# Reordering a two-layer feed-forward stage: upper half of d_ff first, differences cut at a quarter, attention of the next block at later slots

## The chip, the cores and the metric

The kernel runs on one core of a Trainium2 chip. The metric is the time on the device in microseconds (us), taken as the median of several executions. The profile is one such execution seen by the hardware profiler; its span is a little shorter than the time (290.2 us against 291.96 us for the same execution).

The engines are named as in the profile: PE is the matrix engine (PEld is its loading of weights), DVE the vector engine, ACT the scalar engine, POOL the general engine, SP the engine whose queue issues most of the transfers.

## The reference, cut to what matters

Attention inside chunks of 64 rows, and behind it a feed-forward layer with a squared relu:

```
q, k, v: (8, 8, 576, 64)          # batch, heads, sequence, head size
scores = q_chunk @ k_chunk^T / 8  # 64 x 64 for each chunk
attn   = exp(scores - max) / sum
out    = attn @ v_chunk
x = out as (4608, 512)            # tokens, d_model
h = max(x @ w_in, 0)              # w_in  (512, 2048)
y = (h * h) @ w_out               # w_out (2048, 512)
```

Everything comes in as float32; the kernel multiplies in bfloat16 and sums in float32.

## The kernel before

The 4608 tokens are cut into nine blocks of 512, numbered j = 0 to 8; each block consists of two groups of 256 tokens. Blocks 2 to 8 share one form, and the change touches only that form. Such a block is a chain of 30 slots on PE:

- slots 0 to 15: the first layer. In a slot PE multiplies one tile `ft` (128 of the 2048 hidden units) for all 512 tokens, in 4 matmuls of 512 columns; ACT takes the relu, and DVE (for some tiles ACT) squares it into `gT[:, ft, :]`, the left factor of the second layer.
- slots 16 to 29: the second layer, as seven products of half-size blocks in place of eight (a scheme of Strassen's kind). Two slots of 8 matmuls make one product. Some products need `gT` itself, others need a difference of two quarters of it, which DVE forms.

The four quarters of `gT`, by hidden units and tokens, and the differences of them:

```python
def quarters(j):       # a11, a12, a21, a22
    return [gTs[j][:, a:a + HF, c:c + HT] for c in (0, HT) for a in (0, HF)]
# HF = 8 tiles of hidden units, HT = 256 tokens:
# a11: ft 0-7,  tokens 0-255     a12: ft 8-15, tokens 0-255
# a21: ft 0-7,  tokens 256-511   a22: ft 8-15, tokens 256-511
DIFFERENCES = {"d1": (0, 3), "d2": (3, 2), "d5": (0, 1), "d6": (2, 0), "d7": (1, 3)}
EARLY_DIFFERENCES = {8: "d5", 12: "d2"}

def difference(j, name, part):     # part: which of the 8 tiles
    ...
    nc.vector.tensor_tensor(out=state[name, j][:, part], in0=x, in1=y, op=ALU.subtract)

FT_PAIRS = [ft + h for ft in range(n_ft // 2) for h in (n_ft // 2, 0)]
#        = 8, 0, 9, 1, 10, 2, ... 15, 7
```

The first layer. `u` counts the slots, `ft` is the tile of that slot:

```python
for u, (c, n, fts, ft) in enumerate(...):
    h = ps_ffn.tile([128, 512], FP32, name="ps_ffn")          # 4 buffers
    for dt in range(n_dt): nc.tensor.matmul(out=h[:, 0:n], ...)
    ...
    rl = ffn_pool.tile([128, 512], FP32, name="rl", bufs=3)   # bf16 for j < 3
    nc.scalar.activation(out=rl[:, 0:n], in_=h[:, 0:n], func=AF.Relu)
    on_act = SQUARES_ON_ACT_PAIRS if fts is FT_PAIRS else SQUARES_ON_ACT   # (9, 11, 5)
    if (n == 512 and ft in on_act) or ...:
        nc.scalar.activation(out=gT[:, ft, c:c + n], in_=rl[:, 0:n], func=AF.Square)
    else:
        nc.vector.tensor_tensor(out=gT[:, ft, c:c + n], in0=rl, in1=rl, op=ALU.mult)
    if fts is FT_PAIRS and u in EARLY_DIFFERENCES:
        difference(j, EARLY_DIFFERENCES[u], slice(0, HF // 2))
    yield
```

The second layer. `rest_of` forms what is still missing of a difference. The seven products run through two banks of `ps_ffn`, called "n" and "m":

```python
def rest_of(name):
    difference(j, name, slice(HF // 2 if (name, j) in state else 0, HF))
d5 = rest_of("d5")
d2 = rest_of("d2")
yield from product("n", a22, b11_p_b21, True)     # slots 16, 17
... nc.scalar.copy(out=n1, in_=ps)                # ACT
yield from product("m", a11, b12_p_b22, True)     # slots 18, 19
... add(nc.vector, w, ps, n1)                     # DVE
d1 = rest_of("d1")
yield from product("n", d5, b22, False)           # slots 20, 21
... nc.scalar.copy(out=n2, in_=ps)
d6 = rest_of("d6")
yield from product("m", d2, b11, False)           # slots 22, 23
... add(nc.vector, c21, w, ps, ALU.subtract), store
d7 = rest_of("d7")
yield from product("n", d1, b11_m_b22, False)     # slots 24, 25
...
yield from product("m", d6, b11_p_b12, False)     # slots 26, 27
...
yield from product("n", d7, b21_p_b22, False)     # slots 28, 29
```

Between the slots the attention of the next block is woven in, in a plan of slots for its two groups: `SC` scores (64 small matmuls on PE for the two groups, one exponential each on ACT), `AV` values (32 small matmuls in two tiles, and on DVE for each tile a reciprocal and a multiplication), `XT` the transpose of the result by a transfer, `C` and `TD` the cast and transpose of q and k for the block after the next. What is planned at a slot is issued after the relu and square of that slot.

```python
slots = {SC: (6, 6), AV: (9, 13), XT: (12, 16), C: (18, 20), TD: (20, 23)}   # blocks 5, 6, 7
if j == 3:   slots.update({SC: (8, 8), AV: (10, 14), XT: (13, 17)})
elif j == 4: slots.update({SC: (7, 7), AV: (10, 14), XT: (13, 17)})
if j == 2:   slots = {SC: (8, 10), AV: (12, 15), XT: (15, 18), C: (20, 23), TD: (22, 25)}
```

Both `SC` and `AV` use `ps_att`, a pool of 2 buffers: a tile of `AV` waits until the exponential, or the multiplication of the tile two before it, has read its buffer. Block 8 is the last and has no attention woven in.

Of the kernel before, what the change touches and what calls it, by code (L numbers as in the profile page):

```python
# [17 lines left out]
def kernel(  # L18
# [18 lines left out]
    n_ft = d_ff // 128  # L37
# [15 lines left out]
    FIRST_DMA_T = 4  # L53
    FIRST_DMA_X = 6
    SQUARES_ON_ACT = (10, 14, 3)
    SQUARES_ON_ACT_PAIRS = (9, 11, 5)
    BT = GT * max(len(b) for b in blocks)

    const_pool = ctx.enter_context(tc.tile_pool(name="const", bufs=1))
# [132 lines left out]
    state = {}  # L192
# [159 lines left out]
    C, TD = cast_qk, transpose_qk_dma  # L352
    SC, AV, XT = scores, values, transpose_x
# [17 lines left out]
    gTs = {}  # L371
    HF, HD, HT = n_ft // 2, d_model // 2, BT // 2
    DIFFERENCES = {"d1": (0, 3), "d2": (3, 2), "d5": (0, 1), "d6": (2, 0), "d7": (1, 3)}
    EARLY_DIFFERENCES = {8: "d5", 12: "d2"}

    def quarters(j):

        return [gTs[j][:, a:a + HF, c:c + HT] for c in (0, HT) for a in (0, HF)]

    def difference(j, name, part):  # L380
        if (name, j) not in state:
            state[name, j] = wst_pool.tile([128, 1024], FP32, name="w_st").bitcast(BF16).rearrange(
                "p (a f) -> p a f", a=HF)
        x, y = (quarters(j)[i][:, part] for i in DIFFERENCES[name])
        nc.vector.tensor_tensor(out=state[name, j][:, part], in0=x, in1=y, op=ALU.subtract)  # L385
    FT_ORDER = [*range(n_ft // 2, n_ft), *range(n_ft // 2)]

    FT_PAIRS = [ft + h for ft in range(n_ft // 2) for h in (n_ft // 2, 0)]

    def ffn_in(j, parts):  # L390
        if j not in gTs:
            gTs[j] = ffn_pool.tile([128, n_ft, BT], BF16, name="gT")
        gT, xT = gTs[j], xTs[j]
        for u, (c, n, fts, ft) in enumerate((*p, ft) for p in parts for ft in p[2]):
            h = ps_ffn.tile([128, 512], FP32, name="ps_ffn")
            for dt in range(n_dt):
                nc.tensor.matmul(  # L397
                    out=h[:, 0:n],
                    lhsT=w_in_bf[:, dt, ft * 128:(ft + 1) * 128],
                    rhs=xT[:, c // 128:(c + n) // 128, dt, :],  # L400
                    start=(dt == 0), stop=(dt == n_dt - 1))
            if j < 3:
                if n == 512 or u % 2 == 0:
                    rl_tile = ffn_pool.tile([128, 512], FP32, name="rl", bufs=3).bitcast(BF16)
                rl = rl_tile[:, u % 2 * 512:] if n < 512 else rl_tile
            else:
                rl = ffn_pool.tile([128, 512], FP32, name="rl", bufs=3)
            nc.scalar.activation(out=rl[:, 0:n], in_=h[:, 0:n], func=AF.Relu)  # L408
            on_act = SQUARES_ON_ACT_PAIRS if fts is FT_PAIRS else SQUARES_ON_ACT
            if (n == 512 and ft in on_act) or (n < 512 and (j == 0 or ft in (12, 3))):  # L410
                nc.scalar.activation(out=gT[:, ft, c:c + n], in_=rl[:, 0:n], func=AF.Square)  # L411
            else:
                nc.vector.tensor_tensor(  # L413
                    out=gT[:, ft, c:c + n], in0=rl[:, 0:n], in1=rl[:, 0:n], op=ALU.mult)
            if fts is FT_PAIRS and u in EARLY_DIFFERENCES:
                difference(j, EARLY_DIFFERENCES[u], slice(0, HF // 2))
            yield


# [9 lines left out]
    def sum_quarters(out, in0, in1, op=ALU.add, half=slice(None)):  # L429
        return lambda _: add(nc.vector, out[:, half], in0[:, half], in1[:, half], op)  # L430

    def ffn_out(j):
# [6 lines left out]
        a11, a12, a21, a22 = quarters(j)  # L439

        def rest_of(name):
            difference(j, name, slice(HF // 2 if (name, j) in state else 0, HF))
            return state[name, j]

        n_tt = HT // 128
# [55 lines left out]
        d5 = rest_of("d5")  # L501
        d2 = rest_of("d2")
# [8 lines left out]
        d1 = rest_of("d1")  # L511
# [4 lines left out]
        d6 = rest_of("d6")  # L516
        if j == 1:
            d7 = rest_of("d7")
# [5 lines left out]
        if j > 1:  # L524
            d7 = rest_of("d7")
# [19 lines left out]
    def ffn_out_by_ft(j):  # L545

        gT = gTs.pop(j)
        n_tt = len(blocks[j]) * GT // 128
        o_ps = [ps_ffn.tile([128, d_model], FP32, name="ps_ffn") for _ in range(n_tt)]

        def mm(tt, ft):
            nc.tensor.matmul(  # L552
                out=o_ps[tt],
                lhsT=gT[:, ft, tt * 128:(tt + 1) * 128],
                rhs=w_out_bf[:, ft, :],
                start=(ft == 0), stop=(ft == n_ft - 1))


        for ft in range(n_ft - 4):
            for tt in range(n_tt - 1 if ft == 0 else n_tt):  # L560
                mm(tt, ft)
                if ft == 1 and tt == n_tt - 2:
                    mm(n_tt - 1, 0)
            yield
        for tt in range(n_tt):
            for ft in range(n_ft - 4, n_ft):
                mm(tt, ft)
            o_sb = ffn_pool.tile([128, d_model], FP32, name="o_sb", bufs=4)
            nc.scalar.copy(out=o_sb, in_=o_ps[tt])
            b, s0 = chunks[blocks[j][tt // 2]][0]  # L570
            t0 = b * S + s0 + tt % 2 * 128
            nc.gpsimd.dma_start(out=out[t0:t0 + 128, :], in_=o_sb)
            yield
# [49 lines left out]
    for j, grps in enumerate(blocks):  # L623
        nxt = blocks[j + 1] if j + 1 < len(blocks) else []
        far = blocks[j + 2] if j + 2 < len(blocks) else []
        plan = {}

        def at(slot, f, g):
            plan.setdefault(slot, []).append((f, g))

        if j == 0:
            loads, go_slots = itertools.chain(*map(qk_pieces, far)), range(17)
            at(28, sum_quarters(b11_p_b21, b11, b21), None)
            for slot, f in ((24, TA), (27, SC), (29, AV), (31, XT)):
                at(slot, f, nxt[0])
            at(31, TQ, nxt[1])
            at(31, sum_quarters(b11_m_b22, b11, b22, ALU.subtract), None)
            phases = [first_ffn_in, ffn_out_by_ft(0)]
        elif j == 1:
            loads = itertools.chain(*map(v_pieces, nxt), *map(qk_pieces, far))  # L640
            go_slots = [*range(22, 27), *range(28, 48)]
            for slot, f in ((1, TK), (4, SC), (7, AV), (12, XT)):
                at(slot, f, grps[1])
            for i, g in enumerate(nxt):
                for slot, f in ((16 + 4 * i, C), (21 + 6 * i, TD), (36 + i, SC), (38 + 2 * i, AV),
                                (41 + 2 * i, XT)):
                    at(slot, f, g)
            for i, g in enumerate(far):
                at(36 + 4 * i, C, g)
                at(42 + 3 * i, TD, g)  # L650
            at(2, sum_quarters(b11_p_b12, b11, b12), None)
            at(12, sum_quarters(b12_p_b22, b12, b22), None)
            at(20, sum_quarters(b21_p_b22, b21, b22), None)
            phases = [ffn_in(1, [(0, 256, FT_ORDER), (256, 256, FT_ORDER)]), ffn_out(1)]
        else:
            loads, go_slots = pieces(far), range(32)
            slots = {SC: (6, 6), AV: (9, 13), XT: (12, 16), C: (18, 20), TD: (20, 23)}
            if j == 3:
                slots.update({SC: (8, 8), AV: (10, 14), XT: (13, 17)})
                go_slots = [*range(6), *range(13, 32)]  # L660
            elif j == 4:
                slots.update({SC: (7, 7), AV: (10, 14), XT: (13, 17)})
            if j == 2:
                loads = itertools.chain(*map(v_pieces, nxt), loads)
                slots = {SC: (8, 10), AV: (12, 15), XT: (15, 18), C: (20, 23), TD: (22, 25)}
                go_slots = [*range(16), 23, 24, *range(26, 36)]
            for f in (SC, AV, XT):
                for i, g in enumerate(nxt):
                    at(slots[f][i], f, g)
            for f in (C, TD):  # L670
                for i, g in enumerate(far):
                    at(slots[f][i], f, g)
            phases = [ffn_in(j, [(0, BT, FT_PAIRS)]), ffn_out(j)]
        slot = 0
        for phase in phases:
            for _ in phase:
                if slot in go_slots:
                    for f in loads:
                        f()
                        break  # L680
                for f, g in plan.get(slot, []):
                    f(g)
                slot += 1
        assert all(x < slot for x in plan), (j, slot, sorted(plan))
        go(loads)
# [30 lines left out]
```

## Time and profile before

| | |
|---|---|
| time, median of 3 | 291.49 us (291.45 to 292.45) |
| span of the profiled execution | 290.2 us |
| PE busy | 270.4 us, 93% |
| DVE busy | 189.3 us, 65% |
| ACT busy | 162.4 us, 56% |
| squares on DVE, all forms | 130 instructions, 75.1 us |
| differences on DVE | 54 instructions, 49.5 us |
| granted TensorE clock | 1.0 |

How to read a profile of this kind: the page gives busy time and share of each engine; "L413" is line 413 of the kernel; "gT<-rl" says which tile is written from which. In the view of waits a line reads "engine, line <- what it waited for: us in total, times, longest". In the timeline a line gives the start, the length, the engine, the line, the operation and the count of merged instructions, and in square brackets the idle time ahead of it with the instruction that ended it. The view of windows gives the busy time of every engine in stretches of the span.

### The profile page before, as it was taken

The page shows a single profiled execution, that of the slowest core. Times are in us where ns is not written, and L with a number is a line of the kernel's source. Part 1 is how long each engine was busy: PE and PEld are TensorE (multiplying, and loading weights), DVE is VectorE, ACT ScalarE, POOL GpSimd, SP SyncE. Part 2 cuts the span into 40 slices and gives each one's busy share as a digit, 9 for nine tenths or more (in the row PEclk, how much of TensorE's full clock was granted, in tenths as well). Part 3 has the DMA queues.
Part 4 walks back from the last instruction along what each step waited for, and adds up shares of the span by engine and source line. Part 5 has one row for each costly group of instructions (what it writes and reads, how often), then busy time and mean ns, then how long its engine had stood idle before and what let it go on. Part 6 is the DMA issues. An engine that isn't in the chain of part 4 may idle for free.

```text
span 290.2 us, 7184 instructions
## 1 busy us (share of the span) xinstructions
PE 270.4 (93%) x2954; PEld 175.5 (60%) x2954; DVE 189.3 (65%) x317; ACT 162.4 (56%) x277; POOL 55.3 (19%) x92
## 2 busy tenths in 40 slices
PE   2989999999999999999999999799979999799994
PEld 1454445788764586458545854386438744784583
DVE  1256515898934694699359935974497539855882
ACT  1558614884468564864586458463956286118610
POOL 2038843140450002000200020002000300051012
PEclk9999999999999999999999999999999999999999
DMA  7999999999998999999998992479999704232003
GB/s 204 240 335 311 374 333 279 281 226 199 257 226 226 243 206 261 246 210 172 295 255 163 242 285 65 104 160 265 216 200 187 215 20 36 40 93 54 1 24 123
DMA packets 140817, 57.10 MB, mean 197 GB/s; under 512 B 110640, under 2 KB 137520, under 8 KB 140784
## 3 DMA queue, kind: packets, MB, share of 16 engines
q1 hardware_dynamic: 137744, 47.33, 74.2%
q0 software_dynamic: 2896, 9.18, 9.0%
q8 instruction: 23, 0.38, 0.6%
q10 hardware_dynamic: 144, 0.13, 0.1%
q14 instruction: 10, 0.08, 0.1%
HBM read 36.70 MB, written 9.44 MB: 159 GB/s over the span
## 4 chain that ended last, share of the span: by engine, by line
PE 63%; DVE 19%; ACT 7%; issue 4%; SPq 4%; DMA 2%; POOL 0%; DVEq 0%; ACTq 0%
PE ps_ffn L462 30%; PE ps_ffn L397 26%; DVE gT L413 8%; DVE x L326 6%; PE ps_ffn L552 5%; ACT rl L408 4%; DVE w_st L385 3%; ACT e L302 3%; DMA w_st<-in_moe_w_in_dram 2%; SPq L106 1%; SPq L148 1%; DVE rec L325 1%; SPq L152 1%; PE ps_att L345 1%; PE ps_att L291 0%
## 5 line engine op out<-in xcount | busy, mean ns | idle before, releaser
L397 PE MATMUL ps_ffn<-xT,w_in_bf 128*128 128x512 bf16 (+1 forms) x648 | 130.1, 356 | 0.6 <-POOL w_in_bf L170 0.4
L413 DVE TENSOR_TENSOR gT<-rl 128x512 bf16<-128x512 f32 (+2 forms) x130 | 75.1, 606 | 60.7 <-ACT rl L408 59.4
L408 ACT ACTIVATE rl<-ps_ffn 128x512 f32<-128x512 f32 (+2 forms) x162 | 85.8, 549 | 25.7 <-PE ps_ffn L397 24.5
L397 PEld LDWEIGHTS <-w_in_bf 128*128 128x128 bf16 x648 | 61.4, 98 | 57.1 <-POOL w_in_bf L170 0.6
L462 PEld LDWEIGHTS <-w_st 128*128 128x128 bf16 x640 | 62.2, 98 | 7.3
L385 DVE TENSOR_TENSOR w_st<-gT 128x1024 bf16<-128x1024 bf16 (+1 forms) x54 | 49.5, 942 | 0.2
L462 PE MATMUL ps_ffn<-w_out_bf,w_st 128*128 128x256 bf16 x384 | 45.1, 273 | 0.0
L490 POOL DMA_DIRECT2D out_dram<-o_sb x25 | 17.9, 717 | 133.5 <-DVE o_sb L427 128.9
L462 PEld LDWEIGHTS <-gT 128*128 128x128 bf16 x256 | 24.3, 98 | 12.7 <-DVE gT L413 8.5
L462 PE MATMUL ps_ffn<-w_sum,w_st 128*128 128x256 bf16 x256 | 29.6, 273 | 0.0
L542 ACT COPY o_sb<-ps_ffn 128x512 f32<-128x512 f32 (+1 forms) x8 | 4.5, 559 | 41.0 <-PE ps_ffn L462 41.0
L326 DVE TENSOR_TENSOR x<-ps_att,rec 128x512 bf16<-128x512 f32 x36 | 24.9, 692 | 1.2
L462 PE MATMUL ps_ffn<-w_sum,gT 128*128 128x256 bf16 x128 | 16.2, 273 | 5.8 <-DVE gT L413 5.8
L302 ACT ACTIVATE e<-ps_att 128x1024 bf16<-128x1024 f32 x18 | 17.8, 1018 | 6.0 <-PE ps_att L291 6.0
L411 ACT ACTIVATE gT<-rl 128x512 bf16<-128x512 f32 (+2 forms) x32 | 18.5, 577 | 1.0
L462 PE MATMUL ps_ffn<-w_out_bf,gT 128*128 128x256 bf16 x128 | 15.6, 273 | 0.7 <-DVE gT L413 0.7
L552 PE MATMUL ps_ffn<-w_out_bf,gT 128*128 128x512 bf16 x64 | 14.5, 379 | 0.0
L506 ACT COPY n<-ps_ffn 128x512 f32<-128x512 f32 (+1 forms) x9 | 4.8, 539 | 16.9 <-PE ps_ffn L462 16.9
L170 POOL CAST w_in_bf<-w_st 128x512 bf16<-128x512 f32 (+2 forms) x12 | 9.6, 820 | 18.0 <-DMA w_st<-in_moe_w_in_dram 18.0
L318 PEld LDWEIGHTS <-e 64*64 64x64 bf16 x576 | 7.0, 107 | 9.7 <-DVE x L326 2.3
L318 PE MATMUL ps_att<-ve_sb,e 64*64 64x65 bf16 x288 | 9.7, 197 | 1.6 <-DVE x L326 1.4
L259 ACT CAST qkb<-q_sb 128x1024 bf16<-128x1024 f32 x10 | 10.5, 1048 | 0.0
(53 smaller groups left out, 159.7 us busy)
## 6 DMA issues: line engine op xcount, KB each, us to landing
q_sb<-in_q_dram SPq DMA_DIRECT2D x16, 512.0 KB, 6.6
out_dram<-o_sb POOLq DMA_DIRECT2D x29, 256.0 KB, 4.2
k_sb<-in_k_dram SPq DMA_DIRECT2D x24, 256.0 KB, 6.2
ve_sb<-in_v_dram SPq DMA_DIRECT2D x32, 128.0 KB, 4.1
w_st<-in_moe_w_in_dram SPq DMA_DIRECT2D x8, 512.0 KB, 6.2
w_st<-in_moe_w_out_dram SPq DMA_DIRECT2D x8, 512.0 KB, 5.8
vo_sb<-in_v_dram SPq DMA_DIRECT2D x24, 128.0 KB, 4.0
k_sb<-in_k_dram SPq DMA_DIRECT2D x4, 512.0 KB, 7.1
```

Source lines behind the costliest of these rows:

```text
L259: copy(out=qkb[:, 0].rearrange("p (i h d) -> p i h d", i=2, h=H), in_=q_sb.rearrange("p (h i d) -> p i h d", h=H, i=2))
L302: nc.scalar.activation(out=e_out, in_=s_in, func=AF.Exp, scale=scale)
L318: nc.tensor.matmul(out=ps[64 * p:64 * p + 64, a, hp * (D + 1):(hp + 1) * (D + 1)], lhsT=e[64 * c:64 * c + 64, a, hp, t, :], rhs=vb[64 * c: ...
L326: nc.vector.tensor_tensor(out=x[:, t].rearrange("p h a d -> p a h d"), in0=o[:, :, :, 0:D], in1=rec.to_broadcast([128, 2, n_hp, D]), op=AL ...
L385: nc.vector.tensor_tensor(out=state[name, j][:, part], in0=x, in1=y, op=ALU.subtract)
L397: nc.tensor.matmul(out=h[:, 0:n], lhsT=w_in_bf[:, dt, ft * 128:(ft + 1) * 128], rhs=xT[:, c // 128:(c + n) // 128, dt, :], start=(dt == 0) ...
L408: nc.scalar.activation(out=rl[:, 0:n], in_=h[:, 0:n], func=AF.Relu)
L411: nc.scalar.activation(out=gT[:, ft, c:c + n], in_=rl[:, 0:n], func=AF.Square)
L413: nc.vector.tensor_tensor(out=gT[:, ft, c:c + n], in0=rl[:, 0:n], in1=rl[:, 0:n], op=ALU.mult)
L462: nc.tensor.matmul(out=outs[t], lhsT=a[:, i, t * 128:(t + 1) * 128], rhs=b[:, i, :], start=(first and i == 0 and (last or t == 0)), stop=( ...
L490: dma.dma_start(out=out[t0:t0 + HT, col:col + HD].rearrange("(t p) d -> p t d", p=128), in_=o_sb.rearrange("p (t d) -> p t d", d=HD))
L552: nc.tensor.matmul(out=o_ps[tt], lhsT=gT[:, ft, tt * 128:(tt + 1) * 128], rhs=w_out_bf[:, ft, :], start=(ft == 0), stop=(ft == n_ft - 1))
```

## The change

The order of the tiles in the first layer, the cut of the differences, and three slots of the plan are changed together:

- **Order.** Before, upper and lower tiles alternate to the end. After, only tiles 8, 0, 9, 1 come in pairs; then 10 to 15 finish the upper half (done at u = 9), and 2 to 7 come last. The first product of the second layer reads only the upper half, the second product only the lower half.
- **Differences.** Before, half of d5 is formed at u = 8 and half of d2 at u = 12. After, a quarter (tiles 0 and 1) of all five differences is formed at u = 8, where DVE would wait for ACT to finish the exponentials; the rest of each, three quarters, comes where the rest came before.
- **Slots.** In blocks 3 to 7 the scores come at slot 8, the values at 11 and 15, the transposes at 14 and 18. Block 2 keeps its slots.
- **Squares on ACT.** Three of sixteen as before, but all three before slot 8: tiles 9, 10, 12 stand at u = 2, 4, 6; before, tiles 9, 11, 5 stood at u = 2, 6, 11.

```diff
-    SQUARES_ON_ACT_PAIRS = (9, 11, 5)
+    SQUARES_ON_ACT_EARLY = (9, 10, 12)
...
-    EARLY_DIFFERENCES = {8: "d5", 12: "d2"}
...
-    FT_PAIRS = [ft + h for ft in range(n_ft // 2) for h in (n_ft // 2, 0)]
+    N_EARLY = 2
+    FT_EARLY = [ft + h for ft in range(N_EARLY) for h in (n_ft // 2, 0)]
+    FT_EARLY += [ft for ft in FT_ORDER if ft not in FT_EARLY]
...
-            if fts is FT_PAIRS and u in EARLY_DIFFERENCES:
-                difference(j, EARLY_DIFFERENCES[u], slice(0, HF // 2))
+            if fts is FT_EARLY and u == 8:
+                for name in ("d5", "d2", "d1", "d6", "d7"):
+                    difference(j, name, slice(0, N_EARLY))
...
-            difference(j, name, slice(HF // 2 if (name, j) in state else 0, HF))
+            difference(j, name, slice(N_EARLY if (name, j) in state else 0, HF))
...
-            slots = {SC: (6, 6), AV: (9, 13), XT: (12, 16), C: (18, 20), TD: (20, 23)}
+            slots = {SC: (8, 8), AV: (11, 15), XT: (14, 18), C: (18, 20), TD: (20, 23)}
             if j == 3:
-                slots.update({SC: (8, 8), AV: (10, 14), XT: (13, 17)})
                 go_slots = [*range(6), *range(13, 32)]
-            elif j == 4:
-                slots.update({SC: (7, 7), AV: (10, 14), XT: (13, 17)})
```

Nothing is computed that was not computed before, and nothing is left out; `FT_ORDER` is the plain order 8 to 15, 0 to 7, which block 1 uses before and after.

More of the change, by code (lines that the diff above doesn't have):

```diff
@@ L408, in ffn_in @@
             nc.scalar.activation(out=rl[:, 0:n], in_=h[:, 0:n], func=AF.Relu)
-            on_act = SQUARES_ON_ACT_PAIRS if fts is FT_PAIRS else SQUARES_ON_ACT
+            on_act = SQUARES_ON_ACT_EARLY if fts is FT_EARLY else SQUARES_ON_ACT
             if (n == 512 and ft in on_act) or (n < 512 and (j == 0 or ft in (12, 3))):
@@ L672 @@
                     at(slots[f][i], f, g)
-            phases = [ffn_in(j, [(0, BT, FT_PAIRS)]), ffn_out(j)]
+            phases = [ffn_in(j, [(0, BT, FT_EARLY)]), ffn_out(j)]
         slot = 0
```

## The prediction

> **What bounds the kernel now.** I read the page first, then the busy time per block, then the waits of PE, then the timeline of one slow and one fast block. Page and windows (the columns are the stretch, its length, then busy us with counts for PE, PEld, DVE, ACT and POOL, the granted clock, the DMA share and GB/s; the cuts at the first matmul of each block come from the chain of waits; the rows are blocks 2 to 8):
>
> ```profile
> PE 270.4 (93%) x2954; PEld 175.5 (60%) x2954; DVE 189.3 (65%) x317; ACT 162.4 (56%) x277; POOL 55.3 (19%) x92
> ...
> 83.16:111.78 28.62, 28.20 (x305) 18.32 (x304) 17.65 (x33) 18.17 (x28) 4.28 (x7) 1.00 1.04 227
> 111.78:140.14 28.36, 28.00 (x305) 18.09 (x304) 20.83 (x33) 18.06 (x28) 2.86 (x4) 1.00 1.08 230
> 140.14:169.13 28.99, 28.29 (x306) 18.19 (x304) 20.84 (x33) 17.96 (x28) 2.86 (x4) 1.00 1.07 235
> 169.13:199.38 30.25, 28.16 (x305) 18.28 (x304) 20.75 (x33) 18.08 (x28) 2.86 (x4) 1.00 0.64 148
> 199.38:229.62 30.24, 28.14 (x305) 18.25 (x304) 20.75 (x33) 18.08 (x28) 2.86 (x4) 1.00 1.02 225
> 229.62:259.87 30.25, 28.15 (x306) 18.26 (x304) 20.75 (x33) 14.40 (x24) 3.75 (x7) 1.00 0.27 51
> 259.87:290.20 30.33, 26.21 (x177) 16.95 (x174) 18.34 (x30) 13.44 (x25) 4.76 (x8) 1.00 0.18 57
> ```
>
> PE is the bound, but blocks 5, 6 and 7 take 30.25 us where block 3, with the same work, takes 28.36. Where the 1.9 us go, the waits of PE and the timeline of block 6 (PE and DVE mixed from two answers) say:
>
> ```profile
> PE ps_ffn L462 <- DVE gT L413: 6.5, 7, 1.8
> ...
> 208.43 2.32 ACT L408 ACTIVATE rl<-ps_ffn 128x512 f32<-128x512 f32 x4
> ...
> 209.06 1.29 DVE L413 TENSOR_TENSOR gT<-rl 128x512 bf16<-128x512 f32 x2 [3.09 <-ACT rl L408]
> ...
> 214.36 0.69 DVE L385 TENSOR_TENSOR w_st<-gT 128x1024 bf16<-128x1024 bf16 x1
> ...
> 217.25 1.28 DVE L413 TENSOR_TENSOR gT<-rl 128x512 bf16<-128x512 f32 x2
> 217.98 2.62 PEld L462 LDWEIGHTS <-gT 128*128 128x128 bf16 x25 [2.04 <-DVE gT L413]
> 217.99 1.16 PE L462 MATMUL ps_ffn<-w_sum,gT 128*128 128x256 bf16 x9 [1.76 <-DVE gT L413]
> ```
>
> The reader is to see: DVE is idle for 3.09 us while ACT does the exponentials, then works without a gap to 217.9; PE has done 7 matmuls of product n (they need tiles 8 to 14) and stands 1.76 us for tile 15, which in the paired order is squared last but one. Idle first, late afterwards: that is a matter of order, not of load (DVE is busy 20.75 of 30.25 us). Block 3, scores at 8 and values at 10 and 14, has a hole of 1.00 us behind the exponentials and a PE wait of 0.36:
>
> ```profile
> 120.84 0.68 DVE L385 TENSOR_TENSOR w_st<-gT 128x1024 bf16<-128x1024 bf16 x1
> 122.53 1.29 DVE L413 TENSOR_TENSOR gT<-rl 128x512 bf16<-128x512 f32 x2 [1.00 <-ACT rl L408]
> ...
> 130.25 1.16 PE L462 MATMUL ps_ffn<-w_out_bf,gT 128*128 128x256 bf16 x9 [0.36 <-DVE gT L413]
> ```
>
> **What the Trainium skill says.** "VectorE: DVE Perf Modes", section "The perf-mode tier table": a tensor_tensor of two bf16 operands in SBUF runs at two elements a cycle, with fp32 or PSUM operands at one. The trace agrees: 1024 bf16 elements take 0.69 us, 512 from fp32 also 0.69. The same page, section on the TRN2 errata: each operation also pays a fixed cost, so many small ones cost more than one large one. That bears on five quarters; the trace gives the size below. "Perfetto Trace Analysis", section "Per-instruction lifecycle", says that DVE and ACT are strictly first in, first out. The DVE timeline keeps program order, and I build on it: what is issued at u = 8 cannot be overtaken.
>
> **The change, part by part.** I walk block 3, because the new slots are nearly its own, and start at 122.53, where DVE begins the square of u = 9. PE's chain of scores and ACT's exponentials are the same up to there (the third ACT square moves from u = 11 to u = 4, where ACT has 0.27 us of idle time ahead of most relus).
>
> *Differences.* Start to start, 1024 elements take 0.60 us (214.36 to 214.96 in block 6, where the next square follows), 2048 take 1.13 (two of them, merged, take 2.35 us in the timeline, and the second alone 1.22). So 0.53 per 1024 and 0.07 fixed: a quarter (512) 0.33, the rest (1536) 0.87. At u = 8: 5 x 0.33 = 1.67 in place of 0.60, from 120.84 to 122.51. The relu of u = 9 comes at 122.5, so the hole of 1.00 us swallows it. Removed later: 0.60 for d2 at u = 12. Second layer: 2 x 0.87 + 3 x 0.87 = 4.35 in place of 2 x 0.60 + 3 x 1.13 = 4.59.
>
> *DVE after 122.53.* Squares at u = 9 to 15 are now all on DVE: 7 x 0.605 = 4.24 (one more than before). Values twice: 1.69 each (123.74 to 125.43), 3.38. The last square ends at 122.53 + 4.24 + 1.69 = 128.46, since the second values are issued after slot 15. Then values to 130.15, d5 to 131.05, d2 to 131.92, the addition of product m (0.69) to 132.6.
>
> *PE after the scores (120.12).* 3 tiles of 4 x 0.216: 2.60 to 122.72; values 0.39; 4 tiles 3.46 to 126.57; values 0.40 to 126.97; product n 1.79 to 128.76; product m 1.75 to 130.51. Product n needs only tiles squared by 123.2: no wait. Product m's last tile is needed at 129.5, there at 128.5: no wait, 1.0 in hand. The second values' buffers are free at 122.53 + 3 x 0.605 + 1.69 = 126.04, needed at 126.57: no wait. Product d5 has its tiles 0 and 1 early; its third matmul is due at 130.73 and finds d5 at about 131.15 with the semaphore (0.06 between square and matmul in block 3): **a new wait of 0.4**, if dependencies are kept per part of the tile as they are for gT. Then 14 matmuls x 0.109 = 1.53 to 132.68, when the addition of m has just released the bank, and 4 products x 1.745 = 6.98: end at 139.66 where it was 139.98. Block: 28.37 - 0.32 = **28.05**. With no wait at all the same sum gives 27.63, so most of what is there is taken.
>
> *Block by block.* Block 3: -0.3. Block 4: 28.99 to 28.05, -0.95. Blocks 5, 6, 7: 30.25 to 28.05, 3 x -2.2 = -6.6. Block 2 keeps its slots; its squares from bf16 are short (0.36 apart), and its one wait, 0.42 of the second values for the multiplication of the first, ends because d2's half no longer stands in front of it: -0.45. Block 8 has no attention and waits 0.15: -0.1. Sum -8.4: 291.5 - 8.4 = 283.1; I give **283.2**.
>
> **The rivals.** *DVE stays the bound, and the wait only moves to d5.* For it: DVE is gapless from 122.5 to 132.6, and moving the values from 14 to 15 puts 1.69 us straight ahead of d5. Against: product n and m lie between (3.54 us of PE). Each 0.1 us by which DVE slips costs 0.1 in six blocks. If every square, difference and value is delayed so that d5 comes 0.5 later, all blocks take 28.5: 3 us lost, 286. If dependencies are kept for the whole tile, the wait is 0.6 and the time 284.4.
>
> *The bank of m.* Product d2 adds into the bank that the addition on DVE must first read; d2's rest now stands ahead of that addition, 0.87 in place of 0.60. My two ends, 132.6 and 132.68, touch. If it loses 0.2 per block, 1 us: 284.
>
> *ACT or transfers.* Scores at 8 in place of 6 leave less time for the transposes of x (slot 18; 3.4 us to landing, 5.1 at most): issued at about 131, landed by 136, needed at 139.7. The DMA share of 1.07 in blocks 3 and 4 speaks for crowding, yet block 3 already ran XT at 17 without a wait. I expect nothing. The rest of PE at a full clock (1.00 everywhere) has no room to change.
>
> *No gain* would need the wait for gT to return whole as a wait for d5; the 1.8 us of slack that product m brings speaks against it.
>
> **Range and chances.** Best case all waits gone: five blocks at 27.7 and block 2 at 28.0, about 281.3. Bad case, the first rival at half strength with the bank: 285.5. So 281.8 to 285.4 should hold it 8 times in 10. A gain of over 2% means below 285.7: chance 0.87; within 2%: 0.12; slower by over 2%: 0.01, for which a transfer or a new wait would have to cost 14 us over my sum.
>
> **What would show it.** In the windows, blocks 3 to 7 all near 28.05 and alike. In PE's waits, the line for gT (6.5 us) nearly gone, and a new one of product d5 on the differences, about 0.4 each, 2 us in all. On DVE, five differences of 128x512 of about 0.42 us at u = 8, and hardly any idle time between them and the square of u = 9. The first product begins right after the second values. The prediction is wrong if PE waits for values at slot 15 (buffers of ps_att), if the wait for d5 is over 1 us, or if relus of u = 9 to 12 hold up PE through the 4 buffers of ps_ffn behind the exponentials.

## The result, and the profile after

The changed kernel takes 284.41 us (median of 6, 282.58 to 285.65) against 291.78 us (6 runs of the kernel before on the same chips): ratio 0.974, 95% interval 0.969 to 0.978. So it is 2.6% faster, and inside the predicted range. Its executions lie further apart than those of before (3.1 us against 2.0), and that turns out to be a part of the story.

First the page, the waits of PE, and the windows of blocks 2 to 8 in the changed kernel, with the columns as before. The waits are those from 82.8 us on, where block 2 begins; there is only one.

```profile
PE 269.4 (95%) x2954; PEld 175.4 (62%) x2954; DVE 188.6 (67%) x338; ACT 162.1 (57%) x277; POOL 55.8 (20%) x92
```

```profile
PE ps_att L291 <- DMA qkT<-qkb: 1.8, 1, 1.8
```

```profile
82.86:110.86 28.00, 28.00 (x305) 18.25 (x304) 17.66 (x36) 18.15 (x28) 5.27 (x7) 1.00 1.03 223
110.86:138.89 28.03, 27.96 (x305) 18.18 (x304) 20.80 (x36) 17.98 (x28) 2.86 (x4) 1.00 1.09 227
138.89:168.70 29.81, 28.02 (x305) 18.24 (x304) 21.05 (x36) 18.36 (x28) 2.86 (x4) 1.00 1.10 215
168.70:196.73 28.03, 27.96 (x306) 18.20 (x304) 20.79 (x36) 17.99 (x28) 2.86 (x4) 1.00 0.84 192
196.73:224.77 28.04, 27.96 (x305) 18.18 (x304) 20.80 (x36) 17.99 (x28) 2.86 (x4) 1.00 0.94 213
224.77:252.79 28.02, 27.94 (x305) 18.19 (x304) 20.80 (x36) 14.30 (x24) 3.74 (x7) 1.00 0.45 87
252.79:282.80 30.01, 26.04 (x177) 17.03 (x174) 18.61 (x33) 13.45 (x25) 4.76 (x8) 0.97 0.18 57
```

The reader sees three things. The 6.5 us that PE waited for the squares are gone, and so are 1.4 us that it waited for the buffers of the values. Blocks 3 and 5 to 7 are alike, at 28.03 us. Block 4 is not: 29.81, longer than before, with a wait that the kernel before did not have, for a transfer. The spans differ by 290.2 - 282.8 = 7.4 us, and the blocks account for it: block 2 gains 0.62, block 3 0.33, blocks 5 to 7 together 6.65, block 8 0.32, what lies ahead of block 2 0.30, and block 4 loses 0.82. The change does not touch what lies ahead of block 2; over all runs that block starts between 82.3 and 83.3 us.

Inside a block, DVE of block 6 behaves as it was meant to:

```profile
204.59 1.29 DVE L415 TENSOR_TENSOR gT<-rl 128x512 bf16<-128x512 f32 x2 [1.03 <-ACT rl L410]
205.80 1.76 DVE L384 TENSOR_TENSOR w_st<-gT 128x512 bf16<-128x512 bf16 x5
207.49 1.90 DVE L415 TENSOR_TENSOR gT<-rl 128x512 bf16<-128x512 f32 x3
...
215.07 1.82 DVE L384 TENSOR_TENSOR w_st<-gT 128x1536 bf16<-128x1536 bf16 x2
```

The five quarters (1.69 us from start to next start) fill the time of the exponentials, and the squares follow without a gap. PE in the same stretch runs through the products n and m without a wait, and takes 3.74 us from start to start, not 3.49, for the two products behind them; that 0.25 us is the new wait for d5. The list of waits does not show it: the first two matmuls of product d5 use the early quarter, and between the modelled end of the second and the start of the third lie less than 0.1 us:

```profile
213.87 1.91 PE L466 MATMUL ps_ffn<-w_out_bf,gT 128*128 128x256 bf16 x16
215.62 3.91 PE L466 MATMUL ps_ffn<-w_out_bf,w_st 128*128 128x256 bf16 x32
219.36 3.66 PE L466 MATMUL ps_ffn<-w_sum,w_st 128*128 128x256 bf16 x32
```

The wait of block 4 comes out of SP's queue in block 3 (SP's timeline, then PE's line at the scores of block 4):

```profile
134.49 2.84 SPq L268 DMA_TRANSPOSE qkT<-qkb  x1
137.42 0.63 SPq L152 DMA_DIRECT2D vo_sb<-in_v_dram  x1
138.14 6.26 SPq L268 DMA_TRANSPOSE qkT<-qkb  x1
```

```profile
148.82 0.45 PE L291 MATMUL ps_att<-qkT 64*64 64x64 bf16 x32 [1.79 <-DMA qkT<-qkb]
```

The second transpose of q and k starts at 138.14, behind transfers of v that are planned ahead of it, and is issued for 6.26 us; it landed 10.6 us after its start, the longest of its kind in this run. The scores of block 4 need it at 147.0. In the kernel before, the line of the same transpose is:

```profile
138.53 2.76 SPq L268 DMA_TRANSPOSE qkT<-qkb  x1
```

There it landed 5.8 us after its start and was needed at 147.3. So the change did not take time away from this transpose: from its start to its use there are some 8.7 us in both. What differs is how long it took to land.

### The profile page after: what moved, and what is told of

Its sections match the earlier page's. It is cut to its first block, busy times and chain, and to the rows that moved or that the text cites. A ratio compares the mean times of both kernels' runs of the same rounds, so it can differ in the third digit from the quotient of the medians.

```text
span 282.8 us, 7200 instructions
## 1 busy us (share of the span) xinstructions
PE 269.4 (95%) x2954; PEld 175.4 (62%) x2954; DVE 188.6 (67%) x338; ACT 162.1 (57%) x277; POOL 55.8 (20%) x92
## 4 chain that ended last, share of the span: by engine, by line
PE 61%; DVE 15%; DMA 8%; SPq 6%; ACT 5%; issue 3%; POOL 0%; ACTq 0%; DVEq 0%
PE ps_ffn L466 28%; PE ps_ffn L399 25%; DVE gT L415 6%; PE ps_ffn L556 5%; DVE w_st L384 4%; ACT rl L410 4%; DVE x L326 4%; DMA qkT<-qkb 4%; DMA w_st<-in_moe_w_in_dram 3%; SPq L106 2%; DMA k_sb<-in_k_dram 2%; SPq L148 1%; SPq L152 1%; PE ps_att L318 1%; SPq L120 1%
## 5 line engine op out<-in xcount | busy, mean ns | idle before, releaser
L415 DVE TENSOR_TENSOR gT<-rl 128x512 bf16<-128x512 f32 (+2 forms) x130 | 72.7, 593 | 56.1 <-ACT rl L410 55.8
L384 DVE TENSOR_TENSOR w_st<-gT 128x1536 bf16<-128x1536 bf16 (+2 forms) x75 | 50.2, 719 | 0.0
L466 PE MATMUL ps_ffn<-w_out_bf,w_st 128*128 128x256 bf16 x384 | 45.8, 273 | 0.3
L466 PE MATMUL ps_ffn<-w_sum,gT 128*128 128x256 bf16 x128 | 15.3, 273 | 0.0
L291 PEld LDWEIGHTS <-qkT 64*64 64x64 bf16 x576 | 6.1, 110 | 7.9 <-issue 3.6
```

The lines of the kernel that those rows point to most:

```text
L415: nc.vector.tensor_tensor(out=gT[:, ft, c:c + n], in0=rl[:, 0:n], in1=rl[:, 0:n], op=ALU.mult)
L466: nc.tensor.matmul(out=outs[t], lhsT=a[:, i, t * 128:(t + 1) * 128], rhs=b[:, i, :], start=(first and i == 0 and (last or t == 0)), stop=( ...
```

## The experiments

Two questions were open. Which of the three parts of the change pays: the slots, the order, or the quarters? And is the wait of block 4 a price of the change, a chance, or an order in a queue? The table gives the length of the blocks in us, from the first matmul of a block to that of the next, beside the time (the kernel before ran along in every comparison, at 291.8 to 292.0). A wait ahead of a block's first matmul counts to the block before it. The time is the median of all executions.

| kernel | block 2 | 3 | 4 | 5 | 6 | 7 | time | ratio to before, 95% |
|---|---|---|---|---|---|---|---|---|
| before | 28.62 | 28.36 | 28.99 | 30.25 | 30.24 | 30.25 | 291.78 | |
| changed | 28.00 | 28.03 | 29.81 | 28.03 | 28.04 | 28.02 | 284.41 | 0.974 (0.969 to 0.978) |
| e1 slots only | 28.62 | 27.83 | 27.83 | 27.84 | 28.20 | 27.84 | 283.47 | 0.973 (0.968 to 0.978) |
| e2 order, old slots | 28.00 | 28.37 | 30.06 | 30.18 | 30.18 | 30.18 | 292.26 | 1.002 (0.999 to 1.004) |
| e3 no early differences | 28.15 | 28.53 | 28.92 | 28.52 | 28.53 | 28.52 | 285.65 | 0.979 (0.978 to 0.981) |
| e5 v last | 28.07 | 28.04 | 28.03 | 28.03 | 28.03 | 28.03 | 282.83 | 0.969 (0.966 to 0.971) |
| e6 fourth square | 28.01 | 28.17 | 28.00 | 27.79 | 29.76 | 27.79 | 283.39 | 0.966 (0.962 to 0.971) |
| e7 both of these | 27.99 | 27.79 | 27.79 | 27.78 | 27.79 | 27.79 | 281.87 | 0.966 (0.963 to 0.969) |
| e8 slots of block 3 | 28.62 | 28.37 | 28.37 | 28.37 | 28.37 | 28.36 | 285.49 | 0.978 (0.976 to 0.980) |
| e9 slots only, v last | 28.62 | 27.83 | 27.83 | 27.84 | 27.83 | 27.83 | 282.84 | 0.969 (0.968 to 0.971) |

### e1: the slots alone

The kernel before, with nothing changed but the plan:

```diff
-            slots = {SC: (6, 6), AV: (9, 13), XT: (12, 16), C: (18, 20), TD: (20, 23)}
+            slots = {SC: (8, 8), AV: (11, 15), XT: (14, 18), C: (18, 20), TD: (20, 23)}
             if j == 3:
-                slots.update({SC: (8, 8), AV: (10, 14), XT: (13, 17)})
                 go_slots = [*range(6), *range(13, 32)]
-            elif j == 4:
-                slots.update({SC: (7, 7), AV: (10, 14), XT: (13, 17)})
```

> The kernel before with the new slots alone (scores 8, values 11 and 15, transposes 14 and 18 in blocks 3 to 7); pairs to the end, half of d5 at u = 8 and half of d2 at u = 12 as before. Theory A (the whole design is needed: in pairs the first product must still wait for tile 15): blocks 5 to 7 around 28.9 us, time 287 or more. Theory B (the slots alone take the wait away: on DVE there lie between 122.53 and the end of d5 in block 3 six squares, two values and two halves, 8.2 us, against 8.5 us in the changed kernel): first product waits about 0.15 us, no wait for d5, blocks 3 and 5 to 7 at 27.9 to 28.1, time 282.5 to 285 like the changed kernel.

Measured: 283.47 us, no slower than the whole change, and its blocks are shorter, at 27.83 (block 6 has 28.20 because of a wait for a transposed x). From the windows of e1 (blocks 3 and 5) and the waits of its PE from block 2 on, all of them:

```profile
112.11:139.94 27.83, 27.83 (x305) 18.19 (x304) 20.67 (x33) 18.11 (x28) 2.86 (x4) 1.00 1.09 232
...
167.77:195.61 27.84, 27.84 (x305) 18.19 (x304) 20.67 (x33) 18.11 (x28) 2.86 (x4) 1.00 0.84 193
```

```profile
PE ps_att L318 <- DVE x L326: 0.4, 1, 0.4
PE ps_ffn L397 <- DMA xT<-x: 0.2, 1, 0.2
PE ps_ffn L462 <- DVE gT L413: 0.2, 1, 0.2
```

PE is busy for the whole block. The pairs, in which tile 15 is squared last but one, cost nothing here: with the second values behind slot 15, no values stand between the exponentials and that square but the first. Theory B holds; A falls.

### e2: the order and the quarters alone

```diff
-            slots = {SC: (8, 8), AV: (11, 15), XT: (14, 18), C: (18, 20), TD: (20, 23)}
+            slots = {SC: (6, 6), AV: (9, 13), XT: (12, 16), C: (18, 20), TD: (20, 23)}
             if j == 3:
+                slots.update({SC: (8, 8), AV: (10, 14), XT: (13, 17)})
                 go_slots = [*range(6), *range(13, 32)]
+            elif j == 4:
+                slots.update({SC: (7, 7), AV: (10, 14), XT: (13, 17)})
```

> The changed kernel with the slots of before (scores at 6, 7 or 8, values at 9/13 or 10/14): order and quarters alone. Theory A (order frees PE whatever the slots): blocks 5 to 7 at 28.5 or less. Theory B (the slots decide): after the exponentials DVE has nine squares, five quarters and two values, 10.5 us, one gapless run to the end of the first layer; the wait moves from the first product to the second and the blocks 5 to 7 stay at about 30.2, block 4 near 29.9, block 3 about 28.05; time about 290 to 291.

Measured: 292.26 us, as before the change. In blocks 5 to 7 the order does free the first product, and the time comes back as waits elsewhere. DVE of block 5, then lines of PE in the same block:

```profile
178.54 1.29 DVE L415 TENSOR_TENSOR gT<-rl 128x512 bf16<-128x512 f32 x2 [2.86 <-ACT rl L410]
179.75 1.76 DVE L384 TENSOR_TENSOR w_st<-gT 128x512 bf16<-128x512 bf16 x5
```

```profile
183.01 0.22 PE L318 MATMUL ps_att<-ve_sb,e 64*64 64x65 bf16 x2 [0.83 <-DVE x L326]
...
183.85 0.22 PE L318 MATMUL ps_att<-ve_sb,e 64*64 64x65 bf16 x2 [0.51 <-DVE x L326]
...
189.15 1.16 PE L466 MATMUL ps_ffn<-w_out_bf,gT 128*128 128x256 bf16 x9 [0.32 <-DVE gT L415]
```

With the scores at slot 6 DVE idles for 2.86 us through the exponentials, because the square of u = 7 waits for a relu that ACT does behind them. The quarters hang on u = 8, so they come behind that hole instead of in it: 1.69 us more ahead of the first values, whose buffers PE then waits for. I had put the whole loss into the second product; most of it is at the values (4.7 us in the list of waits, against 2.2 for the squares). The length of blocks 5 to 7 was met; the time (290 to 291 expected) was not, and neither was block 3: it was put at 28.05 and takes 28.37, as it does with the old order at the same slots (e8). PE waits 0.41 us there, in the second product, for a square.

### e3: no differences beside the exponentials

```diff
-            if fts is FT_EARLY and u == 8:
+            if False and fts is FT_EARLY and u == 8:
```

> The changed kernel with no difference at u = 8; all five whole in the second layer. If the hole behind the exponentials is what pays for the quarters: DVE idle about 1.0 us behind the exponentials again, d5 1.13 in place of 0.87 at the same start, the wait for d5 about 0.7 us in place of 0.24, blocks 3 and 5 to 7 at 28.5 to 28.6, time about 2.5 us over the changed kernel. If the quarters are of no use: blocks at 28.05, same time.

Measured: 285.65 us, blocks of 28.52 where transfers do not disturb. The hole is empty again and d5 is late (DVE and PE of block 5):

```profile
178.84 1.90 DVE L415 TENSOR_TENSOR gT<-rl 128x512 bf16<-128x512 f32 x3 [1.60 <-ACT rl L410]
```

```profile
187.70 3.67 PE L466 MATMUL ps_ffn<-w_out_bf,w_st 128*128 128x256 bf16 x32 [0.57 <-DVE w_st L384]
```

So within this order the quarters are worth 28.52 - 28.03 = 0.5 us a block: the hole (1.60, longer than the 1.0 that I expected, since I had taken that from a block in which a half of d5 already stood in it) takes them for nothing. The time is 1.2 us above that of the changed kernel, not 2.5 as expected: in its profile the changed kernel loses 1.8 us to a transfer, e3 only 0.4.

### e4: the changed kernel once more

> The changed kernel once more, unaltered. If the 1.8 us that block 4 waits for a transposed qkT is a chance of the transfers, another execution shows another wait in block 4 (0 to 3 us) while blocks 3 and 5 to 7 stay at 28.03; if it is a fixed cost of the change, block 4 is 29.8 again.

Four executions: 282.73, 283.11, 287.69 and 287.72 us. The two upper ones, like one of the four of e6, are left out of the ratio (0.968 to 0.972), and the profile is of one of them: in it the clock granted in block 7 fell to 0.94, and that block took 29.73 us without a wait. Blocks 2 to 5 of the same execution are 28.00 to 28.04 at full clock and block 4 waits for nothing, while the first matmul of block 7 stands 2.8 us for a transposed x. The 1.8 us of block 4 are therefore not a fixed cost. e6, below, shows the same two things at full clock: the transpose of q and k for block 4 starts there at 142.02, lands 4.9 us later and costs 0.2 us, and block 7 waits for x.

### e5: the loads of v behind the transposes

In blocks 3 to 7 of the changed kernel, the loads of q and k (6 or 16 pieces) keep the first slots, and those of v move to slot 24 and later. Blocks 4 to 7 had `range(32)`, so that the loads of v came directly behind those of q and k:

```diff
             if j == 3:
-                go_slots = [*range(6), *range(13, 32)]
+                pass
+            go_slots = [*range(16 if j == 5 else 6), *range(24, 36)]
```

> The changed kernel with the loads of v in blocks 3 to 7 planned at slot 24 and later, behind the transposes of x and qk, instead of ahead of and between them (the loads of q and k stay first). Theory Q (the order in SP's queue: what is urgent, the transposes, stands behind loads that nobody needs for 20 us): the waits of PE for transposed qkT and xT go, all blocks 3 to 7 at 28.03, median 282.5 or less and the executions within 1 us of each other. Theory R (the transfer engines as a whole are full, share 1.1 in blocks 3 and 4): transposes still take up to 10 us to land, block 4 again at 28.5 to 30, spread of 3 us and more.

Measured: 282.83 us, four executions between 282.55 and 282.99; PE waits for no transfer from block 2 on, and blocks 3 to 7 are all 28.03. SP's timeline in block 3 of e5:

```profile
126.49 3.87 SPq L339 DMA_TRANSPOSE xT<-x  x2
130.45 5.12 SPq L268 DMA_TRANSPOSE qkT<-qkb  x2
135.63 1.18 SPq L148 DMA_DIRECT2D ve_sb<-in_v_dram  x2
```

The transposes of q and k start at 130.45 and 133.70 instead of 134.49 and 138.14, with the same work in the engines: the DMA share is 1.12 in block 3, against 1.09. They land after 5.2 and 5.3 us, where the changed kernel took 8.8 and 10.6. Theory R falls: block 4 is not late, the executions lie 0.4 us apart, and the transfer engines were not less loaded. From the start of the first transpose to the landing of the second their share is 1.26 here and 1.18 in the changed kernel. Theory Q holds in that the order of one queue removes the waits. What part of that is the earlier start and what part the shorter landing is not shown; for block 4 either alone would have been enough.

For x the earlier start is what the change had used up. The last transpose of x in block 6 starts 9.7 us ahead of block 7 in the kernel before (first line), 5.5 in the changed kernel (219.09, the second of the two in the second line) and 8.1 in e5:

```profile
219.75 2.26 SPq L339 DMA_TRANSPOSE xT<-x  x1
```

```profile
217.71 2.66 SPq L339 DMA_TRANSPOSE xT<-x  x2
```

With 5.5 us this transpose landed 2.0 us ahead of its use in the changed kernel; in e1, e4 and e6 it came too late.

### e6: a fourth square on ACT

The changed kernel with one more tile squared on ACT:

```diff
-    SQUARES_ON_ACT_EARLY = (9, 10, 12)
+    SQUARES_ON_ACT_EARLY = (9, 10, 12, 5)
```

> The changed kernel with a fourth square on ACT (tile 5, u = 13), where ACT idles 0.27 us ahead of each relu. If the 0.24 us that PE waits for d5 is DVE's load between the exponentials and d5: DVE reaches d5 about 0.3 us earlier, that wait goes, blocks 3 and 5 to 7 at 27.8 in place of 28.03; median about 1 us lower, 281.5 to 284 with what the transfers add. If it is something else: 28.03.

Measured: the blocks that no transfer disturbs are 27.79, the wait for d5 is gone; the time, 283.39 us, hides it behind the transfers. ACT of block 6 takes the square out of its idle time, and PE at the start of block 7 shows what costs more:

```profile
208.54 0.63 ACT L413 ACTIVATE gT<-rl 128x512 bf16<-128x512 f32 x1
```

```profile
224.14 6.22 PE L399 MATMUL ps_ffn<-xT,w_in_bf 128*128 128x512 bf16 x28 [1.80 <-DMA xT<-x]
```

### e7: both

The edits of e5 and e6 together.

> Both together. If both theories hold: blocks 3 to 7 at 27.8, median about 281.5, spread below 1 us. If only the queue's order matters: 282.5; if neither: 283 to 285.

Measured: 281.87 us (281.21 to 282.75), the fastest of all. In the profile PE waits for nothing from block 2 on, and blocks 3 to 7 are 27.79, of which PE is busy 27.79. The spread is 1.5 us, more than I expected; it does not come from these blocks as far as the one profile shows. Against the changed kernel that is 2.5 us less.

### e8: the plan of block 3 for all

```diff
-            slots = {SC: (6, 6), AV: (9, 13), XT: (12, 16), C: (18, 20), TD: (20, 23)}
+            slots = {SC: (8, 8), AV: (10, 14), XT: (13, 17), C: (18, 20), TD: (20, 23)}
             if j == 3:
-                slots.update({SC: (8, 8), AV: (10, 14), XT: (13, 17)})
                 go_slots = [*range(6), *range(13, 32)]
-            elif j == 4:
-                slots.update({SC: (7, 7), AV: (10, 14), XT: (13, 17)})
```

> The kernel before with the plan of its block 3 in blocks 3 to 7 (scores 8, values 10 and 14, transposes 13 and 17): order, halves and squares of before. If it is the scores' move from 6 or 7 to 8 that pays, by letting DVE and ACT finish the tiles ahead of the exponentials: blocks 4 to 7 all at 28.36 as block 3 was, time 291.8 - 0.6 - 3 x 1.9 = 285.5 plus what the transfers add (0 to 3). If the values' move by one slot is what counts: blocks near 29 or more, 288 and up.

Measured: 285.49 us, five blocks of 28.37, and the waits of PE for squares add up to 2.0 us where they were 6.5:

```profile
PE ps_ffn L462 <- DVE gT L413: 2.0, 6, 0.4
```

Scores at slot 8 with values at 10 and 14 are thus 6.4 us of the gain. Block 4 shows the scores by themselves: its values and transposes stand at the same slots in both kernels, and scores at 8 in place of 7 take it from 28.99 to 28.37. In blocks 5 to 7 scores, values and transposes moved together, and their shares are not shown. The step from there to values at 11 and 15 (transposes at 14 and 18) takes another 0.54 from each of five blocks (28.37 to 27.83, e8 to e9): 2.7 us.

### e9: the slots alone, v last

The edits of e1 and of e5's loads together.

> The slots alone (pairs, halves and squares of before) with the loads of v last: the same as e1 without the disturbance of the transfers, to be set against e5. Blocks 3 to 7 at 27.83 against 28.03, block 2 at 28.6 against 28.0, block 8 some 0.1 longer: in sum -0.3 us, time 282.5 against 282.8. If order and quarters are worth what they were made for, this one is 1 us or more slower than e5.

Measured: 282.84 us (282.60 to 283.47), against 282.83 for e5, which differs from it by order, quarters and squares alone. Those three parts are worth nothing in sum that these runs could resolve (each ratio is known to 0.002, some 0.6 us). Taken apart: block 2 gains 0.55 (28.62 to 28.07), block 8 0.35 (from its first matmul to the end of the span 30.49 and 30.14), five blocks lose 0.2 each.

### e10: the kernel before, v last

The loads of e5 in the kernel before.

> The kernel before with the loads of v last and nothing else. There PE waits for no transposed tile; if the order of the queue matters only once PE is ahead, the time stays at 291.5 to 291.8; if it is worth something by itself, it is faster by 0.5 us or more.

Measured: 291.61 us, ratio 1.000 (0.998 to 1.001), and PE waits for squares as it did:

```profile
PE ps_ffn L462 <- DVE gT L413: 6.5, 7, 1.8
```

The order of the queue is worth nothing where PE waits for no transfer, as in the kernel before.

## Why the prediction was right, and where it was not

- **The bound and the walk: right.** Blocks 3 and 5 to 7 were put at 28.05 and are 28.03; the gain in blocks 5 to 7 was put at 6.6 and is 6.65. The sum is nearer than its parts: the 1.77 us by which block 4 missed are offset in part by 0.39 more than expected in blocks 2 and 8 and, by luck, 0.30 ahead of block 2.
- **The new wait for d5: right in kind.** It was put at 0.4 and is 0.24. DVE ended d5 when it was said to (19.45 us into block 3, 19.44 in the walk); PE arrived 0.16 later than in the walk, 19.28 instead of 19.12. The length of the block came out right all the same, because it hangs on DVE's end of d5: what PE took longer it waited less. Without a wait the walk gave 27.63; e6 and e7 show 27.79. The use of the early quarter ahead of the rest shows in the same numbers: d5 ends 0.4 us after product d5 has begun.
- **"I expect nothing" of the transfers: wrong.** The rival was named and dismissed on the ground that block 3 had run its transposes at slot 17 without a wait. That was true of x in a block of 28.36 us. The transpose that came late was that of q and k, which I had not walked at all. It had no less time than before (some 8.7 us from start to use in both), but this time it took 10.6 us to land instead of 5.8; why it did stays open. The transposes of x for block 7 did lose time to the change, 9.7 us to 5.5, and are late in e1, e4 and e6. The wait of block 4 cost 1.79 us in the profiled execution, and all waits for transfers together 284.41 - 282.83 = 1.6 us in the median by e5.
- **Block 4: wrong for that reason**, -0.95 predicted, +0.82 measured; by e5 it is 28.03, as walked.
- **Blocks 2 and 8: mis-sized.** -0.45 and -0.1 were taken from the waits in the list (0.42 and 0.15); the gain is 0.62 and 0.32. The list counts from the modelled end of the matmul before. In block 8 of the kernel before, 7 matmuls from 273.52 at 0.11 us end at 274.29, the next starts at 274.60: 0.31 lost, 0.15 listed. In e3 the list says 0.56 to 0.57 and the block is 28.52 - 27.79 = 0.73 longer than the block without waits.
- **What the prediction left unsaid.** It gave one sum for three parts, and its reading ("a matter of order, not of load") let the order of the tiles look like the cure. e1, e2 and e9 show that the order that matters is that of the attention's work on DVE and ACT, set by the slots; "order, not load" holds in that sense. The changed order of the tiles pays only in blocks 2 and 8, and gives that back in the others.

What stays open: why e7's executions are 1.5 us apart, and why one transpose took 10.6 us to land. A kernel with pairs in blocks 3 to 7 and the new order in blocks 2 and 8 was not tried.

## What to carry to other kernels

When several edits act on one wait, take the work between two fixed points on the limiting side engine for each edit alone (here 8.2 us against 8.5 from the end of the exponentials to d5): that sum told ahead of e1 that one part was enough. When a change pulls the bounding engine ahead, walk the transfers of every kind again from their place in the queue to their use, not only those that the change moves; put what is needed soonest first, and let loads wait that nobody needs for a block. A wait in PE's list was less than what it cost here each time that it was compared (0.15 for 0.31 us, 0.42 for 0.62, 0.56 for 0.73).

## What was not expected of the hardware

A transpose by transfer was issued for 6.26 us and landed 10.6 us after its start in the changed kernel, where the median of its kind was 6.3 us and that of the kernel before 5.1; the DMA share of blocks 3 and 4 was hardly different (1.09 and 1.10, against 1.08 and 1.07). In e5 two such transposes landed in 5.2 and 5.3 us at a share of 1.26. The share did not tell which transfer would be late.
